# A DFT and two feed-forward layers on one core: six chunks of x have their halves summed by the transfers that load them

## The chip, the core and the metric

The kernel runs on one core of a Trainium2 chip. The metric is the device time of one execution in microseconds (us). The engines go by the names of the profile: PE is TensorE's matmul side and PEld its weight load, DVE is VectorE, ACT ScalarE, POOL GpSimd, SP the SyncE queue from which nearly all transfers are issued. A small q behind a name (SPq, ACTq) is the engine's sequencer, which issues and waits.

## What is computed

x has 2 sequences of 3008 rows of 256 numbers. The output is a real part of a two-dimensional DFT, followed by two feed-forward layers:

```python
X = np.fft.fft(x, axis=1)
X = np.fft.fft(X, axis=2)
x = X.real.reshape(6016, 256)
h = x @ moe_w_in;  x = (h * (1.0 / (1.0 + np.exp(-h)))) @ moe_w_out
h = x @ moe2_w_in; y = (h * np.clip(h + 3.0, 0.0, 6.0) / 6.0) @ moe2_w_out
```

The hidden width of each layer is 2048, and the weights are given in float64.

## The kernel before

**Stages.** The DFT over the 3008 rows is split as 47 x 64. Step 1 (`step1`) does the 47-point part, step 2 the DFT over the 256 columns, step 3 the 64-point part; the result lies in the tile `eo` (even and odd parts). Symmetries are used up ahead of step 1: each row is added to its mirror row, and each half of the columns to the other half and subtracted from it. These adds are called folds here. Then the first layer runs over chunks of 502 tokens (`win1`, `win1_end`, `parts`, `low`), and the second one.

**Chunks of x.** x is loaded in 11 chunks (the table `XCH`, line 60), numbered 0 to 10: 0 to 5 belong to the first sequence, 6 to 10 to the second. Their widths in columns are 1, 2, 4, 4, 4, 2 and 3, 4, 4, 4, 2. A column is 96 rows (48 for each of two halves, spread over partitions) of four parts of 128 numbers, which are the row, its mirror and both with the columns mirrored. `load_x` (line 316) issues one load for chunks 0 and 1 and two for every later one, of 64 and of 32 partitions, all on SP. There are four buffers; chunk i uses buffer i mod 4, and the load of chunk i + 4 is issued behind step 1 of chunk i.

**Folds.** `fold` (line 322) does three operations on VectorE: the first fold adds parts 2 and 3 to parts 0 and 1 (line 325), the second ones make the sum and the difference of parts 0 and 1 (lines 328 and 329). Chunk 2 (`HALF_FOLDED`) has only the first; its second folds are done by TensorE, with two matmuls for each one (lines 349, 350) and a negated table in `t1_sb`. `step1_next` folds chunk i + 1 ahead of the matmuls of chunk i.

**What sets the order.** The order is written out by hand (the schedule is manual): each engine runs its instructions in program order, and semaphores hold it where data are missing. The loop `while i < nx` puts `steps23(g)`, which is step 2 of tile g, step 3 of tile g - 1 and the evacuation of tile g - 2, between the chunks of the second sequence. Then `while g < 14` does the last tiles, and has the first products of the first layer among them. `busy` and the matmuls on `nil` are fillers: they compute nothing that is used.

**Around the change.** The raw float64 weights (`load_raw`, 1 MB each) are issued on SP behind the loads of x. They are decoded on VectorE by `bits_to_float32`, a step at a time, as `advance` gives out time. `split` makes the rounded part `xhi` of a token chunk on ScalarE and puts the rest, `xlo` (line 184, on VectorE), on a list; `do_later` empties it. Before, `do_later` runs in every turn of the last loop right behind `steps23(g)`. In `win1` VectorE makes `z` (`zg`, line 542) of the first product, in `win1_end` it makes `h` (line 553); from g = 8 on it adds to the step 2 tile `o2` (line 387), which step 3 (line 397) reads.

Of the kernel before, what the change touches and what calls it, by code (L numbers as in the profile page):

```python
# [36 lines left out]
F32 = mybir.dt.float32  # L37
# [20 lines left out]
XB = 4  # L58
HALF_FOLDED = 2
XCH = [(0, 0, 1), (0, 1, 2), (0, 3, 4), (0, 7, 4), (0, 11, 4), (0, 15, 2)]  # L60
# [16 lines left out]
def body(tc, xh, x128, t1, t2, t3, w1, w128, w2, out):  # L77
# [227 lines left out]
    w128_raw = fft.tile([P, NF, 2], U32, name="w128_raw")  # L305
    t1_sb = fft.tile([P, 6 * 104], F32, name="t1_sb")
    t2_sb = fft.tile([P, 257], F32, name="t2_sb")
# [5 lines left out]
    xt = {}  # L313
    xbuf = [xp.tile([P, XB, 4 * P], F32, name=f"x{i}", tag=f"x{i}") for i in range(4)]

    def load_x(i):
        n, c, k = XCH[i]
        xt[i] = xbuf[i % len(xbuf)]
        for at in (slice(0, P, 2), slice(1, P, 4)) if i > 1 else (slice(None),):
            nc.sync.dma_start(xt[i][at, :k, :], xh[at, n, c : c + k, :])  # L320

    def fold(i):
        k = XCH[i][2]
        x = xt.pop(i)[:, :k]
        V.tensor_tensor(out=x[:, :, 0:256], in0=x[:, :, 0:256], in1=x[:, :, 256:512], op=ALU.add)
        if i == HALF_FOLDED:
            return x
        V.tensor_tensor(out=x[:, :, 256:384], in0=x[:, :, 0:128], in1=x[:, :, 128:256], op=ALU.add)
        V.tensor_tensor(out=x[:, :, 384:512], in0=x[:, :, 0:128], in1=x[:, :, 128:256], op=ALU.subtract)
        return x  # L330

# [6 lines left out]
    def step1(i, x):  # L338
        n, c, k = XCH[i]
        for h in range(2):  # L340
            ps = psX.tile([P, XB, 96], F32, name="ps1", tag=f"s{h}")
            src = x[:, :, 256 + 128 * h : 384 + 128 * h]
            if SLOTS[c] == 0:
                T.matmul(ps[:, 0, :], src[:, 0], t1_sb[:, 192 + 96 * h : 288 + 96 * h], start=True, stop=False)
                T.matmul(ps[:, 0, 0:48], src[:, 1], t1_sb[:, 384 + 48 * h : 432 + 48 * h], start=False, stop=True)
                k, j = 1, 0
            elif i == HALF_FOLDED:
                for m in range(k):
                    T.matmul(ps[:, m, :], x[:, m, 0:128], t1_sb[:, 96 * h : 96 * h + 96], start=True, stop=False)
                    T.matmul(ps[:, m, :], x[:, m, 128:256], t1_sb[:, 528 * h : 528 * h + 96], start=False, stop=True)  # L350
                j = SLOTS[c]
            else:
                for m in range(k):
                    T.matmul(ps[:, m, :], src[:, m], t1_sb[:, 96 * h : 96 * h + 96], start=True, stop=True)  # L354
                j = SLOTS[c]
            A.activation(
                out1[n][:, h, :, :, j : j + k], ps[:, :k, :].rearrange("p n (s q) -> p q s n", s=2), AF.Copy
            )
# [56 lines left out]
    G.memset(nil, 0.0)  # L415
    G.memset(xbuf[3], 0.0)
    for i in range(2):
        G.memset(xbuf[i][:, XCH[i][2] :], 0.0)
    V.memset(three, 3.0)
# [4 lines left out]
    V.memset(minus, -1.0)  # L424
    V.memset(minus[0:1], 0.0)
    nx = len(XCH)
    for i in range(4):
        load_x(i)
# [8 lines left out]
    def step1_next():  # L437

        nonlocal folded, i
        x = folded  # L440
        if i + 1 < nx:
            folded = fold(i + 1)
        step1(i, x)
        if i + 4 < nx:
            load_x(i + 4)
        if i + 4 == nx - 1:
            load_raw(1, w1, 0)
        i += 1
        if i == 1:
            nc.sync.dma_start(t2_sb, t2)  # L450
            nc.sync.dma_start(t3_sb, t3)
            nc.sync.dma_start(w128_raw, w128)
        if i < HALF_FOLDED + 1:
            busy(3)
        if i == 3:
            V.tensor_tensor(out=xl[:, 0], in0=xl[:, 0], in1=xl[:, 1], op=ALU.add)
        if i == 5:
            step1_last()
        if i == nx - 4:
            load_raw(1, w1, 1)  # L460
            advance(steps, 1)
# [108 lines left out]
    while g < 14:  # L570
        if g < 12:
            steps23(g)
        do_later()
        if g in (7, 10):
# [340 lines left out]
def tables():  # L915
# [6 lines left out]

    t1 = np.zeros((P, 2 * 96 + 2 * 96 + 2 * 48 + 48 + 96))
    r0, r1 = rows()
# [6 lines left out]
    for i in range(2):  # L931
        t1[r0, 480 + 24 * i : 492 + 24 * i] = co[:, i::2]
        t1[r0, 492 + 24 * i : 504 + 24 * i] = si[:, i::2]
        t1[r1, 492 + 24 * i : 504 + 24 * i] = co[:, i::2]
    t1[:, 528:624] = -t1[:, 96:192]
    d, l = np.arange(P), np.arange(P + 1)
# [15 lines left out]
def layout_x(x):  # L952
# [3 lines left out]
    r = rows()  # L956
    xh = np.zeros((P, B, NJ + 1, 4, P), x.dtype)
    xl = np.zeros((P, 2, B, 2, NB // 2), x.dtype)
    for c, j in enumerate(SLOTS):
        for half in range(2 if j < NJ else 1):  # L960
            b = j + NJ * half if j < NJ else NB // 2
            s = (NB * a + NA * b) % S
            for n in range(B):
# [74 lines left out]
```

## Time and profile before

| | us |
|---|---|
| median of 3 runs | 959.12 (959.12 to 960.47) |
| profiled execution | 959.21 |
| its span (first to last instruction) | 957.3 |
| PE busy | 940.8 (98%) |
| DVE busy | 671.4 (70%) |
| ACT busy | 643.6 (67%) |
| POOL busy | 536.7 (56%) |

All times of the trace are counted from the start of the span. A line of the timeline gives the start, the duration (from the first to the last of a group), the engine, the line of the code, the operation, what it writes and reads, and the count. Square brackets tell how long the engine had been idle before it, and what released it. A wait is put down to the release that came last. A float32 matmul appears as two.

### The profile page before, as it was taken

Reading aid. Unit: us, or ns where it says so; the run is one execution under the profiler, and the core shown is the slowest. Engines: PE = TensorE matmul, PEld = TensorE weight load, DVE = VectorE, ACT = ScalarE, POOL = GpSimd, SP = SyncE. Lnnn points to the kernel's source line nnn. Section 1 sums busy time; section 2 is a strip of 40 time slices with the busy share of each in tenths; the row PEclk is TensorE's granted clock in tenths of the full one; section 3 lists DMA queues with packets and bytes.
Section 4 is the critical chain, followed back from the end, with each engine's and each line's share of the span. In section 5 each row is a group of like instructions: output and inputs, shape, how many; then the busy total and the mean of one; then the engine's idle time right before and its main releaser. Section 6 shows DMA issues by size and latency. Waiting matters only on the chain.

```text
span 957.3 us, 12077 instructions
## 1 busy us (share of the span) xinstructions
PE 940.8 (98%) x4292; PEld 778.5 (81%) x4292; DVE 671.4 (70%) x923; ACT 643.6 (67%) x1122; POOL 536.7 (56%) x393
## 2 busy tenths in 40 slices
PE   8999999999999999999999999999999999999998
PEld 8977788888788788888788878888888888888886
DVE  7899999889989897564567675555555555555543
ACT  3777767666656666565677677766776677677665
POOL 1046655646556475465575567754664674576543
PEclk9999999999999999999999999999999999999999
DMA  8433221224252414186400002020020002001001
GB/s 298 170 125 125 92 99 44 99 104 164 83 201 105 158 61 158 64 318 247 150 6 39 1 1 86 1 87 1 1 74 14 1 1 86 1 0 44 1 1 43
DMA packets 20585, 80.23 MB, mean 84 GB/s; under 512 B 2246, under 2 KB 9036, under 8 KB 17900
## 3 DMA queue, kind: packets, MB, share of 16 engines
q1 hardware_dynamic: 20380, 79.14, 22.9%
q8 instruction: 33, 0.54, 0.2%
q10 hardware_dynamic: 144, 0.32, 0.1%
q14 instruction: 28, 0.23, 0.1%
HBM read 50.85 MB, written 28.60 MB: 83 GB/s over the span
## 4 chain that ended last, share of the span: by engine, by line
PE 87%; DVE 8%; issue 3%; ACT 2%; DMA 1%; SPq 0%; DVEq 0%
PE y L295 16%; PE y L297 16%; PE y L296 16%; PE ab L296 4%; PE ab L295 4%; PE ab L297 4%; PE pa L295 3%; PE pa L296 3%; PE pa L297 3%; PE pb L296 2%; PE pb L295 2%; PE pb L297 2%; PE ps L354 1%; PE pc L295 1%; PE pc L296 1%
## 5 line engine op out<-in xcount | busy, mean ns | idle before, releaser
L769 POOL TENSOR_TENSOR glo<-h,ghi 128x502 fp32r<-128x502 f32 (+1 forms) x192 | 250.3, 1315 | 198.7 <-ACT ghi L766 194.9
L604 POOL TENSOR_TENSOR glo<-h,ghi 128x502 fp32r<-128x502 f32 (+1 forms) x144 | 222.7, 1563 | 209.9 <-ACT h L563 180.5
L295 PE MATMUL y<-ghi,whi 128*128 128x502 f32 (+1 forms) x768 | 300.7, 392 | 4.8 <-DVE st L640 2.8
L297 PE MATMUL y<-ghi,wlo 128*128 128x502 f32 (+1 forms) x768 | 300.4, 391 | 0.0
L296 PE MATMUL y<-glo,whi 128*128 128x502 f32 (+1 forms) x768 | 300.4, 391 | 0.0
L295 PEld LDWEIGHTS y<-ghi,whi 128*128 128x128 f32 x768 | 145.3, 189 | 37.5 <-ACT h L563 3.6
L296 PEld LDWEIGHTS y<-glo,whi 128*128 128x128 f32 x768 | 145.4, 189 | 30.7 <-POOL glo L604 0.2
L297 PEld LDWEIGHTS y<-ghi,wlo 128*128 128x128 f32 x768 | 144.9, 189 | 30.2
L766 ACT ACTIVATE ghi<-h 128x502 fp32r<-128x502 f32 (+1 forms) x192 | 118.0, 624 | 49.8 <-DVE h L761 49.8
L562 ACT ACTIVATE ghi<-ab 128x502 fp32r<-128x502 f32 (+1 forms) x96 | 56.6, 590 | 120.9 <-DVE h L553 119.8
L761 DVE SCALAR_TENSOR_TENSOR h<-h,pc 128x502 f32<-128x502 f32 (+1 forms) x96 | 65.1, 678 | 72.2 <-ACT h L758 72.2
L875 DVE TENSOR_TENSOR pc<-u,pb 128x502 f32<-128x502 f32 (+1 forms) x48 | 32.9, 685 | 102.8 <-ACT u L812 102.8
L812 ACT ACTIVATE u<-pa 128x502 f32<-128x502 f32 (+1 forms) x96 | 56.7, 590 | 56.4 <-PE pa L297 55.8
L758 ACT ACTIVATE h<-pc,three 128x502 f32<-128x502 f32 (+1 forms) x96 | 64.6, 673 | 41.7 <-DVE pc L875 37.0
L295 PE MATMUL ab<-xhi,whi 128*128 128x502 f32 (+1 forms) x192 | 75.6, 394 | 1.8 <-DVE zs L542 0.9
L542 DVE SCALAR_TENSOR_TENSOR zs<-eb,w_sb,ab 128x502 f32<-128x502 f32 (+1 forms) x80 | 58.4, 730 | 25.3 <-PE ab L297 25.3
L296 PE MATMUL ab<-xlo,whi 128*128 128x502 f32 (+1 forms) x192 | 75.2, 392 | 0.2 <-DVE xlo L184 0.2
L297 PE MATMUL ab<-xhi,wlo 128*128 128x502 f32 (+1 forms) x192 | 74.9, 390 | 0.0
L758 ACT ACTIVATE h<-pd,three 128x502 f32<-128x502 f32 (+1 forms) x96 | 64.8, 675 | 1.1 <-DVE pd L887 1.1
L761 DVE SCALAR_TENSOR_TENSOR h<-h,pd 128x502 f32<-128x502 f32 (+1 forms) x96 | 64.4, 671 | 0.8 <-ACT h L758 0.8
L563 ACT ACTIVATE h<-h 128x502 f32<-128x502 f32 (+1 forms) x96 | 60.0, 625 | 3.0
L562 ACT ACTIVATE ghi<-h 128x502 fp32r<-128x502 f32 (+1 forms) x96 | 60.2, 627 | 0.0
(173 smaller groups left out, 1586.3 us busy)
## 6 DMA issues: line engine op xcount, KB each, us to landing
raw<-in_w SPq DMA_DIRECT2D x16, 1024.0 KB, 6.5
u<-y_d SPq DMA_DIRECT2D x6, 1004.0 KB, 4.8
part_d<-st SPq DMA_DIRECT2D x5, 1004.0 KB, 4.4
st<-part_d SPq DMA_DIRECT2D x5, 1004.0 KB, 6.4
y_d<-st SPq DMA_DIRECT2D x5, 1004.0 KB, 5.0
out<-st SPq DMA_DIRECT2D x10, 502.0 KB, 3.1
x<-in_xh SPq DMA_DIRECT2D x7, 512.0 KB, 4.6
w2h_d<-h SPq DMA_DIRECT2D x7, 512.0 KB, 2.6
```

The costliest lines, as they stand in the source:

```text
L295: T.matmul(o, wh, xhi, start=first, stop=False, **group)
L296: T.matmul(o, wh, xlo, start=False, stop=False, **group)
L297: T.matmul(o, wl, xhi, start=False, stop=last, **group)
L542: V.scalar_tensor_tensor(out=z[:, :n], in0=eb[:, :n], scalar=w128_sb[:, f : f + 1], in1=ab[:, :n], op0=ALU.mult, op1=ALU.add)
L562: A.activation(ghi[:, s, :n], src, AF.Silu)
L563: A.activation(h[:, s, :n], src, AF.Silu)
L604: eng.tensor_tensor(out=glo[:, s, :n], in0=h[:, s, :n], in1=ghi[:, s, :n], op=ALU.subtract)
L758: A.activation(h[:, i, :n], c[:, :n], AF.Relu, bias=three)
L761: V.scalar_tensor_tensor(out=h[:, i, :n], in0=h[:, i, :n], scalar=6.0, in1=c[:, :n], op0=ALU.min, op1=ALU.mult)
L766: A.activation(g[0][:, i, :n], h[:, i, :n], AF.Copy)
L769: G.tensor_tensor(out=g[1][:, i, :n], in0=h[:, i, :n], in1=g[0][:, i, :n], op=ALU.subtract)
L812: A.activation(t[:, :n], pa[:, :n], AF.Copy)
```

## The change

Chunks 3 to 8 (`SUMMED`) are loaded in two steps. First parts 0 and 1 go into the buffer, then parts 2 and 3 are added to them in SBUF by a transfer with `accum_op=ALU.add`, which GpSimd issues. Such a sum waits until the first half has landed. x is laid out anew in HBM for it, the two halves of a chunk apart. VectorE then does only the second folds of these chunks. They write into the other half of the buffer, so that matmuls read one half and the next load goes into the other. Chunk 2 is folded wholly on VectorE; its doubled matmuls and the negated table go.

Chunks 0 and 1 have small buffers of their own now, and chunks 2 to 10 go around four of full size, so six chunks are under way at the start. The first half of chunk 3 is issued on ScalarE's queue. A third group of filler matmuls stands behind chunk 2. `do_later` runs only at the end of the turns g = 9 and g = 11.

```diff
@@ load_x, fold
-    xbuf = [xp.tile([P, XB, 4 * P], F32, name=f"x{i}", tag=f"x{i}") for i in range(4)]
+    xbuf = [xp.tile([P, 2, k, 2 * P], F32, name=f"x{i}", tag=f"x{i}") for i, k in enumerate((1, 2, *[XB] * 4))]
...
-        xt[i] = xbuf[i % len(xbuf)]
-        for at in (slice(0, P, 2), slice(1, P, 4)) if i > 1 else (slice(None),):
-            nc.sync.dma_start(xt[i][at, :k, :], xh[at, n, c : c + k, :])
+        xt[i] = xbuf[i if i < 2 else 2 + (i - 2) % 4]
+        halves = [slice(0, 1), slice(1, 2)] if i in SUMMED else [slice(0, 2)]
+        for h in halves:
+            for at in (slice(0, P, 2), slice(1, P, 4)) if i > 1 else (slice(None),):
+                dst, src = xt[i][at, slice(0, h.stop - h.start), :k, :], xh[at, n, h, c : c + k, :]
+                if h.start:
+                    G.dma_start(dst, src, accum_op=ALU.add)
+                else:
+                    (A if i == SUMMED[0] else nc.sync).dma_start(dst, src)
...
-        x = xt.pop(i)[:, :k]
-        V.tensor_tensor(out=x[:, :, 0:256], in0=x[:, :, 0:256], in1=x[:, :, 256:512], op=ALU.add)
-        if i == HALF_FOLDED:
-            return x
-        V.tensor_tensor(out=x[:, :, 256:384], in0=x[:, :, 0:128], in1=x[:, :, 128:256], op=ALU.add)
-        V.tensor_tensor(out=x[:, :, 384:512], in0=x[:, :, 0:128], in1=x[:, :, 128:256], op=ALU.subtract)
-        return x
+        x, y = (xt[i][:, h, :k] for h in range(2))
+        if i not in SUMMED:
+            V.tensor_tensor(out=x, in0=x, in1=y, op=ALU.add)
+        V.tensor_tensor(out=y[:, :, 0:128], in0=x[:, :, 0:128], in1=x[:, :, 128:256], op=ALU.add)
+        V.tensor_tensor(out=y[:, :, 128:256], in0=x[:, :, 0:128], in1=x[:, :, 128:256], op=ALU.subtract)
+        return y
@@ step1
-            elif i == HALF_FOLDED:
-                for m in range(k):
-                    T.matmul(ps[:, m, :], x[:, m, 0:128], t1_sb[:, 96 * h : 96 * h + 96], start=True, stop=False)
-                    T.matmul(ps[:, m, :], x[:, m, 128:256], t1_sb[:, 528 * h : 528 * h + 96], start=False, stop=True)
-                j = SLOTS[c]
@@ the start
-    G.memset(xbuf[3], 0.0)
-    for i in range(2):
-        G.memset(xbuf[i][:, XCH[i][2] :], 0.0)
+    G.memset(xbuf[3][:, 0], 0.0)
+    G.memset(xbuf[5], 0.0)
...
+    V.memset(xbuf[4][:, 0], 0.0)
-    for i in range(4):
+    for i in range(6):
         load_x(i)
@@ step1_next
-        if i + 4 < nx:
+        if 2 <= i < nx - 4:
             load_x(i + 4)
...
-        if i < HALF_FOLDED + 1:
+        if i < 4:
             busy(3)
@@ while g < 14
         if g < 12:
             steps23(g)
-        do_later()
...
+        if g in (9, 11):
+            do_later()
         advance(steps, 1700 if g < 8 else 1400)
```

On VectorE, the folds of chunks 2 to 4 before (the tiles x0 to x3 are the four buffers; chunk 4 is in x0):

```order
L325 TENSOR_TENSOR x2_138<-x2_138 128x4x256
L325 TENSOR_TENSOR x3_139<-x3_139 128x4x256
L328 TENSOR_TENSOR x3_139<-x3_139 128x4x128
L329 TENSOR_TENSOR x3_139<-x3_139 128x4x128
L456 TENSOR_TENSOR xl_132<-xl_132 128x128
L325 TENSOR_TENSOR x0_136<-x0_136 128x4x256
L328 TENSOR_TENSOR x0_136<-x0_136 128x4x128
L329 TENSOR_TENSOR x0_136<-x0_136 128x4x128
```

and the same place after it (chunk 4 is in x4):

```order
L332 TENSOR_TENSOR x2_138<-x2_138 128x1024
L333 TENSOR_TENSOR x2_138<-x2_138 128x4x128
L334 TENSOR_TENSOR x2_138<-x2_138 128x4x128
L333 TENSOR_TENSOR x3_139<-x3_139 128x4x128
L334 TENSOR_TENSOR x3_139<-x3_139 128x4x128
L456 TENSOR_TENSOR xl_132<-xl_132 128x128
L333 TENSOR_TENSOR x4_140<-x4_140 128x4x128
L334 TENSOR_TENSOR x4_140<-x4_140 128x4x128
```

Chunk 2 has gained its two second folds, chunks 3 and 4 have lost the first one.

On SP, the loads of chunks 5 to 9 before (buffers x1, x2, x3, x0, x1):

```order
L320 DMA x1_137<-in_xh 64x1024
L320 DMA x1_137<-in_xh 32x1024
L320 DMA x2_138<-in_xh 64x1536
L320 DMA x2_138<-in_xh 32x1536
L320 DMA x3_139<-in_xh 64x2048
L320 DMA x3_139<-in_xh 32x2048
L320 DMA x0_136<-in_xh 64x2048
L320 DMA x0_136<-in_xh 32x2048
L320 DMA x1_137<-in_xh 64x2048
L320 DMA x1_137<-in_xh 32x2048
```

and on GpSimd after it, the sums of chunks 3 to 8 (buffers x3, x4, x5, x2, x3, x4), which stand between its memsets and its first subtractions:

```order
L324 DMA x3_139<-in_xh 64x1024
L324 DMA x3_139<-in_xh 32x1024
L324 DMA x4_140<-in_xh 64x1024
L324 DMA x4_140<-in_xh 32x1024
L324 DMA x5_141<-in_xh 64x512
L324 DMA x5_141<-in_xh 32x512
L324 DMA x2_138<-in_xh 64x768
L324 DMA x2_138<-in_xh 32x768
L324 DMA x3_139<-in_xh 64x1024
L324 DMA x3_139<-in_xh 32x1024
L324 DMA x4_140<-in_xh 64x1024
L324 DMA x4_140<-in_xh 32x1024
```

SP loaded whole chunks, whose rows are twice as long; now it loads the first halves, and GpSimd has twelve transfers that it didn't have.

On VectorE, around the first products of the first layer (42 to 53 us in the trace before), before:

```order
L387 TENSOR_TENSOR o2_526<-ps2_525,xr_133 128x2x129
L184 TENSOR_TENSOR xlo0_517<-eo_75,xhi0_516 128x1004
L126 TENSOR_SCALAR lo1_1_448<-hi1_1_447 128x1024
L128 SCALAR_TENSOR_TENSOR lo1_1_448<-raw_1_1_313,lo1_1_448 128x1024
L387 TENSOR_TENSOR o2_543<-ps2_542,xr_133 128x2x129
...
L387 TENSOR_TENSOR o2_592<-ps2_591,xr_133 128x2x129
L184 TENSOR_TENSOR xlo1_576<-eo_75,xhi1_575 128x1004
L553 SCALAR_TENSOR_TENSOR h_605<-zg0_582,ab_581 128x502
L542 SCALAR_TENSOR_TENSOR zg0_582<-eb0_518,w128_sb_71,ab_611 128x502
```

and after it:

```order
L387 TENSOR_TENSOR o2_532<-ps2_531,xr_133 128x2x129
L126 TENSOR_SCALAR lo1_1_454<-hi1_1_453 128x1024
L128 SCALAR_TENSOR_TENSOR lo1_1_454<-raw_1_1_320,lo1_1_454 128x1024
L387 TENSOR_TENSOR o2_548<-ps2_547,xr_133 128x2x129
L184 TENSOR_TENSOR xlo0_523<-eo_75,xhi0_522 128x1004
...
L387 TENSOR_TENSOR o2_598<-ps2_597,xr_133 128x2x129
L553 SCALAR_TENSOR_TENSOR h_610<-zg0_588,ab_587 128x502
L542 SCALAR_TENSOR_TENSOR zg0_588<-eb0_524,w128_sb_71,ab_616 128x502
L184 TENSOR_TENSOR xlo1_582<-eo_75,xhi1_581 128x1004
```

xlo0 has moved behind the o2 of g = 9, and xlo1 behind the first h and the second zg.

## Rows read from the trace of the kernel before

**Rows 1.** Busy time of each engine over the span, from the page (share, instructions).

```profile
PE 940.8 (98%) x4292; PEld 778.5 (81%) x4292; DVE 671.4 (70%) x923; ACT 643.6 (67%) x1122; POOL 536.7 (56%) x393
```

**Rows 2.** Busy us by stretch: PE, PEld, DVE, ACT, POOL; clock, transfer share, GB/s.

```profile
10.00:14.00 4.00, 3.91 (x36) 3.77 (x34) 2.98 (x5) 0.98 (x2) 0.00 (x0) 1.00 0.90 328
14.00:18.00 4.00, 3.37 (x43) 3.06 (x41) 3.53 (x6) 1.66 (x4) 0.00 (x0) 1.00 0.81 262
18.00:22.00 4.00, 3.91 (x34) 3.67 (x32) 3.84 (x7) 2.29 (x8) 0.00 (x0) 1.00 0.92 307
26.00:30.00 4.00, 4.00 (x39) 4.00 (x38) 3.76 (x7) 2.44 (x8) 0.00 (x0) 1.00 0.99 395
30.00:34.00 4.00, 4.00 (x39) 4.00 (x38) 3.63 (x9) 4.00 (x10) 0.00 (x0) 1.00 0.14 55
38.00:42.00 4.00, 4.00 (x38) 4.00 (x37) 2.96 (x4) 4.00 (x10) 0.00 (x0) 1.00 0.53 200
```

**Rows 3.** Timeline of the start, 1 to 18 us, all engines.

```profile
1.23 1.76 DVE L414 MEMSET x<- 128x2048 f32 x1 [1.23 <-PEq L1026]
...
3.05 0.20 ACT L421 ACTIVATE mask<-three 128x1 f32<-128x1 f32 x1 [0.61 <-DVE three L419]
...
4.74 0.43 DVE L325 TENSOR_TENSOR x<-x 128x256 f32<-128x256 f32 x1 [1.11 <-DMA x<-in_xh]
...
7.95 1.22 DVE L325 TENSOR_TENSOR x<-x 128x1024 f32<-128x1024 f32 x1 [0.45 <-DMA x<-in_xh]
...
8.19 0.86 PE L336 MATMUL psw<-nil 128*128 128x128 f32 x6
...
9.28 0.43 PE L349 MATMUL ps<-t_sb,x 128*128 128x96 f32 x2 [0.23 <-issue]
...
13.15 2.00 PE L354 MATMUL ps<-t_sb,x 128*128 128x96 f32 x16
...
14.98 0.69 DVE L328 TENSOR_TENSOR x<-x 128x512 f32<-128x512 f32 x1
...
15.78 2.00 PE L354 MATMUL ps<-t_sb,x 128*128 128x96 f32 x16 [0.63 <-ACT out L356]
```

**Rows 4.** Loads of x: by size with us to landing; then all 20.

```profile
x<-in_xh SPq DMA_DIRECT2D x1, 192.0 KB, 3.4
x<-in_xh SPq DMA_DIRECT2D x9, 256.0 KB, 4.0
L320 SPq DMA_DIRECT2D x<-in_xh x20: 395/591/1106, 0.7 to 22.2; - x20
DMA to landing us min/median/max: 3.4/4.3/6.1
```

**Rows 5.** Timeline, chunks 6 and 7 and the first weight tile.

```profile
18.19 0.95 DVE L325 TENSOR_TENSOR x<-x 128x768 f32<-128x768 f32 x1
...
23.50 1.92 PE L354 MATMUL ps<-t_sb,x 128*128 128x96 f32 x16
...
29.97 1.14 ACT L110 ACTIVATE lo<-raw 128x1024 f32<-128x1024 f32 x1 [0.44 <-DMA raw<-in_w]
```

**Rows 6.** Timeline of the first products, 42 to 66 us, VectorE and TensorE.

```profile
42.89 1.20 DVE L184 TENSOR_TENSOR xlo<-eo,xhi 128x1004 fp32r<-128x1004 f32 x1
...
46.43 1.13 PE L397 MATMUL ps<-t_sb,o 128*128 128x128 f32 x8 [1.11 <-DVE o L387]
...
47.63 0.39 PE L296 MATMUL ab<-xlo,whi 128*128 128x502 f32 x1
...
48.29 0.74 DVE L542 SCALAR_TENSOR_TENSOR zg<-eb,w_sb,ab 128x502 f32<-128x502 f32 x1 [1.06 <-PE ab L297]
...
51.24 1.06 PE L397 MATMUL ps<-t_sb,o 128*128 128x128 f32 x8
...
53.16 0.49 PE L295 MATMUL ab<-xhi,whi 128*128 128x502 f32 x1 [0.86 <-DVE zg L542]
...
65.48 0.74 DVE L542 SCALAR_TENSOR_TENSOR zs<-eb,w_sb,ab 128x502 f32<-128x502 f32 x1 [1.15 <-PE ab L297]
```

More of the change, by code (lines that the diff above doesn't have):

```diff
@@ L58 @@
 XB = 4
-HALF_FOLDED = 2
+SUMMED = range(3, 9)
 XCH = [(0, 0, 1), (0, 1, 2), (0, 3, 4), (0, 7, 4), (0, 11, 4), (0, 15, 2)]
@@ L305, in body @@
     w128_raw = fft.tile([P, NF, 2], U32, name="w128_raw")
-    t1_sb = fft.tile([P, 6 * 104], F32, name="t1_sb")
+    t1_sb = fft.tile([P, 4 * 96 + 144], F32, name="t1_sb")
     t2_sb = fft.tile([P, 257], F32, name="t2_sb")
@@ L341, in step1 @@
             ps = psX.tile([P, XB, 96], F32, name="ps1", tag=f"s{h}")
-            src = x[:, :, 256 + 128 * h : 384 + 128 * h]
+            src = x[:, :, 128 * h : 128 * h + 128]
             if SLOTS[c] == 0:
@@ L921, in pair @@
         return np.stack([first, second], axis=2).reshape(NA, QA)
-    t1 = np.zeros((P, 2 * 96 + 2 * 96 + 2 * 48 + 48 + 96))
+    t1 = np.zeros((P, 2 * 96 + 2 * 96 + 2 * 48 + 48))
     r0, r1 = rows()
@@ L934, in tables @@
         t1[r1, 492 + 24 * i : 504 + 24 * i] = co[:, i::2]
-    t1[:, 528:624] = -t1[:, 96:192]
     d, l = np.arange(P), np.arange(P + 1)
@@ L956, in layout_x @@
     r = rows()
-    xh = np.zeros((P, B, NJ + 1, 4, P), x.dtype)
+    xh = np.zeros((P, B, 2, NJ + 1, 2, P), x.dtype)
     xl = np.zeros((P, 2, B, 2, NB // 2), x.dtype)
@@ L975, in layout_x @@
                 for part, y, idx in parts:
-                    xh[r[half], n, c, part] = y[:, idx]
+                    xh[r[half], n, part // 2, c, part % 2] = y[:, idx]
                     if idx is minus:
-                        xh[r[half], n, c, part, 0] = 0.0
-    return xh.reshape(P, B, NJ + 1, 4 * P), xl
+                        xh[r[half], n, part // 2, c, part % 2, 0] = 0.0
+    return xh.reshape(P, B, 2, NJ + 1, 2 * P), xl
 def token_columns():
```

## The prediction

> **What bounds the kernel now.** I read the page first: TensorE is busy 98% of the 957.3 us span and VectorE 70% [rows 1]. The change touches only the first 55 us, so the page says little more than this: behind the start the kernel is a TensorE kernel, and whatever TensorE gains or loses in the start should stay to the end. Then the busy time by stretch: in the first four stretches shown, between 10 and 30 us, the transfer engines are busy 81 to 99% of the time and move 262 to 395 GB/s [rows 2]. So the loads of x are themselves near a limit, and a change that gives those engines more to do is not free by default. Third, the start in order of time [rows 3]: chunk 2 lands at 7.95, VectorE folds it once, and TensorE does the second fold by doubled matmuls from 9.28 until chunk 3 follows at 13.15. At 15.78 TensorE has waited 0.63. Chunks 6 to 8 stand in [rows 5]: the matmuls of chunk 7 start at 23.50, without a wait, and the first weight decode waits for its transfer at 29.97. From 18 to 42 us TensorE has next to no idle time, so a chunk that comes late there is a direct loss. Last, the end of the start [rows 6]: TensorE waits 1.11 us at 46.43 for an o2 tile that VectorE makes behind xlo0, and 0.86 at 53.16 for zg, which VectorE makes behind xlo1.
>
> **The change, part by part. Work on VectorE.** The first folds of chunks 3 to 8 go: four of 1.22 (4 columns), one of 0.95 (3 columns), one of 0.69 (2 columns), 6.5 us. Chunk 2 gets two second folds, 0.69 and about the same, 1.4 us [rows 3, 5]. The zeroing of the chunk 4 buffer, half of a 1.76 us memset, or 0.88, falls in the 1.11 us in which VectorE waits for chunk 0, so it is hidden; without that cover it would delay chunk 0 by 0.88 [rows 3]. The relief of 5 us is not on the path: in the start TensorE waits for data and itself.
>
> **TensorE.** Chunk 2 takes 2.00 us (as chunk 3) instead of 13.15 - 9.28 = 3.87. It starts 0.69 later, behind its second fold, and three more filler matmuls follow it, a group of 0.86 (three float32 matmuls are six in the trace). So chunk 3 has its turn at 9.28 + 0.69 + 2.00 + 0.86 = 12.83, 0.3 us earlier than now, and if chunk 4 is there too the 0.63 us wait goes: at most 1.0 us are to be won [rows 3].
>
> **The summing transfers.** No row shows one, nor a transfer issued by GpSimd. The nearest are the plain loads of x: 0.59 us to issue, 3.4 to 6.1 us to landing, median 4.3; the 192 KB pieces 3.4, the 256 KB ones 4.0 [rows 4]. I call the time from issue to landing L. Each chunk of the six now has two of them in a row: first half, landing, GpSimd issues the sum, landing. Chunk 3: the ScalarE queue issues its pieces behind the table load and mask, at 3.3 and 3.9 [rows 3], the sums follow 0.6 apart, so its last sum lands at 3.9 + L + 0.6 + L. Chunk 4 has its first half under way from the beginning as well, and its turn comes 2 us later, so it isn't the tight one. Chunk 7 is: it reuses chunk 3's buffer, so SP holds its load until both second folds (1.37) have read that buffer. Its matmuls can start at 3.9 + 2L + 0.6 + 1.37 + 0.6 + 2L + 0.6 + 0.74 = 7.8 + 4L, the 0.74 being the fold ahead of them. It is wanted at 23.50 [rows 5]. With L = 3.4 it comes 2.1 us early, with 4.3 it is 1.5 late, with 6.1 it is 8.7 late; it is just in time at 3.9. The pieces are now 256 and 128 KB, half of what they were, and a sum has to read what it adds to; I take 3.7 for a plain half and 4.1 for a sum, by the rows of 192 and 256 KB. That gives 23.4: no loss and no gain. Behind SP's wait for chunk 3 stand the loads of chunks 8 to 10 and then the weights, so the same lateness would go on to those. On GpSimd only the first glo stands behind the sums, which needs products of 50 us and later; on ScalarE the evacuation of chunk 0 stands behind its two issues, and chunk 0 isn't folded before 4.74, when these are done [rows 3].
>
> A transfer from GpSimd has its first byte at about 1 us, one from SP or ScalarE at 0.6, says the Trainium skill (DMA: Bandwidth & Descriptors, Latency and other measured facts); no row here shows the former. By it, an estimate, the two sums on chunk 7's path would cost 0.4 us more each and the result would be 0.8 us higher than mine.
>
> **The weights behind them.** The first raw weight tile is issued behind chunk 10, and its user on ScalarE waits 0.44 for it, until 29.97 [rows 5]. ScalarE is busy without a gap from 30 to 34 and from 38 to 42 us, so lateness passes through [rows 2]. The sums add into 21 columns x 96 rows x 1 KB = 2.06 MB. If reading those again costs as much as moving them, that is 5.2 us at the 395 GB/s of 26 to 30 us; what was left unused between 10 and 22 us, (67 + 133 + 88) GB/s x 4 us = 1.15 MB, or 2.9 us, can take some of it [rows 2]. So the bounds are 0 and +2.3 us. I take 0: the loads are issued earlier and fill the gaps that the four buffers left. For the same reason I book no gain of the start: what TensorE wins before 20 us it would wait for at the weights.
>
> **The later xlo.** do_later now runs once after steps23(9) and once behind the products of g = 11. xlo0 goes behind the o2 of g = 9: that o2 is ready 1.11 us earlier (the length of xlo0 on the chain), and TensorE's wait of 1.11 goes. xlo0 itself ends at about 46.25 instead of 44.1, when the first product with xlo0 is due at 46.52 (47.63 - 1.11), so it is hidden; that cover is 0.3 us thick, and what xlo0 is later than that is lost. xlo1 goes behind h and zg. They now start as soon as TensorE has its product, so the 0.86 us wait at 53.16 goes as well. TensorE's last work before it, the step of 51.24, moves by 1.11 and bounds the gain: 1.11 + 0.86 = 1.97, 2.0 us. Does it last? VectorE itself wins only the 1.06 us in which it waited at 48.29. But at 65.48 VectorE waits 1.15 for TensorE, so it is VectorE that has slack there, more than the 0.9 it is behind [rows 6]. I keep 2.0; the bounds are 1.1 (the first wait alone) and 2.2 (with the last of xlo's waits).
>
> **Sum.** The profiled execution took 959.21 us (its span 957.3 and 1.9 around it), the median is 959.12: no difference that matters. 0 for the loads, 0 for the weights, -2.0 for the later xlo: 957.2, and against the median 957.1.
>
> **Rivals.** (a) *Sums as quick as small loads.* With L = 3.4 throughout, all of the 1.0 us of the start stays if the weights also come earlier: 959.1 - 2.0 - 1.0 = 956.1; the smaller pieces and six chunks in flight speak for it, the 90% busy transfer engines against. (b) *The start eats the gain.* L = 4.3 to 4.7, or the full 2.3 us at the weights: +1.5 to +3.1 less 2.0, so 958.6 to 960.2. The median landing speaks for it. (c) *Slower: two landings in series, twice.* The place is chunk 7, behind chunk 3 on one buffer. If plain halves take 4.3 and sums 8.6, chunk 7 is ready at 7.8 + 2 x 4.3 + 2 x 8.6 = 33.6, 10.1 us late, and 959.1 + 10.1 - 2.0 = 967.2. It decides from a mean L of 4.9 (+3.9 less 2.0).  For it: the engines are nearly full as it is. Against it: a landing is mostly time in the queue, and queues get shorter when pieces are halved.
>
> An add in a transfer reads two sources for each write and so runs at half a copy's rate, by the Trainium skill (Collectives: The Full Stack, The bandwidth ceiling: the fold count and why AG ≠ RS ≠ AR). It is the rule that speaks against this change and leads to (c); no row here shows a sum, so nothing yet agrees or disagrees.
>
> **Chances.** Forecast, 956.5 to 957.8: 0.38. (a) 0.24, (b) 0.15, (c) 0.23. A measurement of this kernel can tell about 0.2%, 1.9 us, from no change: the line is at 957.2, in the middle of the forecast. So faster is (a) and half of the forecast, 0.43; within 0.2% the other half and (b), 0.34; slower (c), 0.23. The range runs from 955.0, some way below (a), to 963.0, into the near part of (c); beyond it lie some 0.05 below and 0.12 above.
>
> **What would show it.** In the profile after: o2 and its step3 at about 45.3 without a wait, and no wait for zg at 53 (the 2.0). Chunk 3's matmuls at about 12.8 to 13.2 and chunk 7's at about 23.4, neither behind a wait of VectorE for a sum of more than 0.5 us. L of the sums near 4. ScalarE's wait for the raw tile at 29.97 no longer than 0.44. I am wrong if VectorE waits for sums in chunks 3 to 8 and TensorE idles behind it, or if the gain at 46 and 53 us comes back as new waits for VectorE before 90 us.

## The result and the profile after

The change makes the kernel slower: 965.0 us (964.28 to 965.48) against 959.49 us of the kernel before beside it, a ratio of 1.0055 with an interval of 1.0038 to 1.0073. The forecast was 957.1 with a range up to 963.0, so the time lies outside it, on the side of rival (c). The profiled execution took 964.28 us with a span of 962.5, 5.2 us more than before.

The busy line of the page, against [rows 1]:

```profile
PE 944.5 (98%) x4282; PEld 781.5 (81%) x4282; DVE 667.9 (69%) x920; ACT 643.9 (67%) x1122; POOL 545.1 (57%) x404
```

VectorE has 3.5 us less to do and GpSimd 8.4 us more, as the change says. The next view shows where the time went. It has the stretches of [rows 2] and the same columns (busy us of PE, PEld, DVE, ACT, POOL; granted clock, share of the transfer engines, GB/s):

```profile
10.00:14.00 4.00, 3.27 (x27) 2.91 (x26) 1.61 (x3) 1.00 (x3) 3.51 (x4) 1.00 1.01 210
14.00:18.00 4.00, 2.53 (x18) 2.56 (x18) 2.79 (x5) 0.51 (x2) 0.00 (x0) 0.85 0.97 221
18.00:22.00 4.00, 4.00 (x40) 3.88 (x39) 0.94 (x3) 1.71 (x4) 3.51 (x4) 0.72 0.84 214
22.00:26.00 4.00, 2.88 (x22) 2.46 (x22) 1.03 (x2) 1.71 (x6) 1.71 (x2) 1.00 0.98 207
```

The transfer engines are as busy as before or busier (1.01 and 0.97 against 0.90 and 0.81), yet they move 210 and 221 GB/s where it was 328 and 262. TensorE is idle for 1.5 us of the second stretch and 1.1 us of the fourth, and between 14 and 22 us its granted clock is below 1.00 on average. The same in order of time, against [rows 3] and [rows 5] (start, duration, engine, line, operation; in brackets the idle time ahead of it and its releaser):

```profile
9.09 1.23 DVE L332 TENSOR_TENSOR x<-x 128x1024 f32<-128x1024 f32 x1 [1.56 <-DMA x<-in_xh]
...
11.14 2.00 PE L354 MATMUL ps<-t_sb,x 128*128 128x96 f32 x16 [0.57 <-issue]
...
14.63 0.69 DVE L333 TENSOR_TENSOR x<-x 128x512 f32<-128x512 f32 x1 [2.99 <-DMA x<-in_xh]
...
15.47 5.41 PE L354 MATMUL ps<-t_sb,x 128*128 128x96 f32 x32 [1.63 <-DVE x L333]
...
23.93 0.56 DVE L333 TENSOR_TENSOR x<-x 128x384 f32<-128x384 f32 x1 [2.55 <-DMA x<-in_xh]
...
24.63 1.55 PE L354 MATMUL ps<-t_sb,x 128*128 128x96 f32 x12 [1.12 <-DVE x L333]
...
26.81 0.69 DVE L333 TENSOR_TENSOR x<-x 128x512 f32<-128x512 f32 x1 [1.85 <-DMA x<-in_xh]
...
27.83 1.92 PE L354 MATMUL ps<-t_sb,x 128*128 128x96 f32 x16
...
34.26 1.19 ACT L110 ACTIVATE lo<-raw 128x1024 f32<-128x1024 f32 x1
```

The trace before has for the matmuls of chunks 6 and 8:

```profile
20.37 1.48 PE L354 MATMUL ps<-t_sb,x 128*128 128x96 f32 x12
...
27.07 1.92 PE L354 MATMUL ps<-t_sb,x 128*128 128x96 f32 x16
```

Read the lines after the change from the top: chunk 2's first fold (7.95 before), its matmuls (9.28), chunk 3's fold and its matmuls with those of chunk 4 (13.15), chunk 6's fold and matmuls (20.37), chunk 7's (23.50), and the first weight decode (29.97). Every fold of a summed chunk waits for its transfer. The lateness is 1.9 us at chunk 2, 2.3 at chunk 3, and 4.3 at chunks 6 and 7. From there it is handed on: the product `y` that begins 240 us into the trace before comes about 5 us later, and the last one of the kernel 4.9 us later.

The transfers themselves, against [rows 4]: issue times in ns (shortest, median, longest), first and last start, and the time from issue to landing. L324 are the sums, L326 the plain loads:

```profile
L324 POOL DMA_DIRECT2D x<-in_xh x12: 842/1090/1842, 7.3 to 23.8; - x12
...
  DVE x L333: 11.3, 6
...
DMA to landing us min/median/max: 5.0/5.9/7.4
...
L326 SPq DMA_DIRECT2D x<-in_xh x18: 455/571/742, 0.7 to 26.7; - x18
...
DMA to landing us min/median/max: 2.7/4.7/6.0
```

The second line says who waited for the sums: VectorE's second folds, six times, 11.3 us in all. Last, what each queue's packets cost in the first 45 us (packets, MB, share of 16 engines' time; q0 is GpSimd's queue, q1 that of SP; ScalarE's is a third one, with 0.66 MB):

```profile
q1 hardware_dynamic: 2800, 7.52, 46.7%
q0 software_dynamic: 768, 2.07, 26.5%
```

A plain MB takes 6.2% of the engines' time in this stretch, a summed one 12.8%, 2.06 times as much. The Trainium skill (Collectives: The Full Stack, The bandwidth ceiling: the fold count and why AG ≠ RS ≠ AR) says of the add in a collective that it needs two source reads and runs at about half a copy's rate, and the trace agrees for this add. The new layout of x costs no engine time by itself: before, SP's queue took 66.8% for 10.63 MB, 6.3% for one.

### The profile page after: what moved, and what is told of

The parts are those of the page before. It is cut to its first block, busy times and chain, and to the rows that moved or that the text cites. A ratio compares the mean times of both kernels' runs of the same rounds, so it can differ in the third digit from the quotient of the medians.

```text
span 962.5 us, 12083 instructions
## 1 busy us (share of the span) xinstructions
PE 944.5 (98%) x4282; PEld 781.5 (81%) x4282; DVE 667.9 (69%) x920; ACT 643.9 (67%) x1122; POOL 545.1 (57%) x404
## 3 DMA queue, kind: packets, MB, share of 16 engines
q0 software_dynamic: 768, 2.07, 1.2%
## 4 chain that ended last, share of the span: by engine, by line
PE 86%; DVE 8%; issue 2%; DMA 2%; ACT 1%; POOL 0%; DVEq 0%; POOLq 0%
PE y L295 16%; PE y L296 16%; PE y L297 16%; PE ab L295 4%; PE ab L296 4%; PE ab L297 4%; PE pa L295 3%; PE pa L296 3%; PE pa L297 3%; PE pb L296 2%; DMA x<-in_xh 2%; PE pb L295 2%; PE pb L297 2%; PE pc L295 1%; PE pc L296 1%
```

## The experiments

The theory after this profile: the sums take longer to land and take the engines twice as long, and chunks 6 and 7, which need two such round trips in a row, come 4.3 us late. The rivals: GpSimd's queue is slow whatever it carries; the reuse of four buffers is the trouble; six chunks under way at once delay the one that is needed first; TensorE's lower clock adds to it; and the order of `xlo` costs something on its own.

### The sums apart from their add

```diff
-                    G.dma_start(dst, src, accum_op=ALU.add)
+                    G.dma_start(dst, src)
```

> The changed kernel with the twelve GpSimd transfers as plain copies: they overwrite the first half, so the first fold of chunks 3 to 8 is left out; issue, waits and sizes stay. Theory A (a summed byte costs the transfer engines twice a plain one, and they are full): the GpSimd queue takes per MB about what SP's takes (6.2% of the first 45 us instead of 12.8%), landings fall from 5.9 to about 4.3, chunk 7's matmuls start near 25 instead of 27.83, total about 960. Theory B (the delay is that of two landings in series and of GpSimd's slow issue, whatever the transfer does): landings stay above 5 us, chunk 7 stays near 27.5, total 964 to 965.

Measured: 960.85 us (959.6 to 963.55), a ratio of 1.0028 [1.0019, 1.0037]. Its queue in the first 45 us, the issues with their landing, and the matmuls of chunk 6:

```profile
q0 software_dynamic: 672, 2.07, 14.3%
...
L324 POOL DMA_DIRECT2D x<-in_xh x12: 537/549/702, 7.2 to 22.3; - x12
...
DMA to landing us min/median/max: 3.5/4.2/5.3
...
22.77 1.55 PE L354 MATMUL ps<-t_sb,x 128*128 128x96 f32 x12 [1.09 <-DVE x L333]
```

The same 2.07 MB on the same queue cost 14.3% of the engines without the add and 26.5% with it, a factor of 1.85; they land after 4.2 us instead of 5.9 and are issued in 0.55 us instead of 1.09. So the engine time is that of the add, not of GpSimd's queue. But chunk 6 is still 2.4 us late (22.77 against 20.37), and chunk 7, at 25.97, comes between the two forecasts of 25 and 27.5: some half of the loss is there without any add. The two landings in series and the six chunks under way are left in this kernel.

### The whole change without the new order of xlo

```diff
         if g < 12:
             steps23(g)
+        do_later()
...
-        if g in (9, 11):
-            do_later()
```

> The changed kernel with do_later in its old place. If the move is worth 2.0 us in the changed kernel: 967. If it is given back there: 965 to 965.5, with the waits for o2 (1.1) and zg (0.9) back at about 50 and 57 us and the wait of 1.39 at 61.76 gone.

Measured: 964.93 us, a ratio of 1.0072 [1.006, 1.0085]; the interval overlaps that of the whole change. TensorE's line for chunk 6, and a stretch behind it:

```profile
24.60 2.26 PE L354 MATMUL ps<-t_sb,x 128*128 128x96 f32 x12 [2.08 <-DVE x L333]
...
26.00:28.00 2.00, 2.00 (x12) 2.00 (x11) 1.15 (x2) 0.54 (x3) 0.00 (x0) 0.50 1.04 307
```

Chunk 6's matmuls start as in the changed kernel, and the products are 5.9 us late from the first one on. So the start alone makes the loss. This profile shows one thing more. The folds of chunk 7 begin when they did (26.85 against 26.81), but its matmuls start at 29.43, 1.6 us later than in the changed kernel: TensorE had done chunks 3 and 4 at full clock, waited 2.08 us for chunk 6 instead of 1.12, and behind this wait its clock fell to 0.50.

### The new order of xlo alone

```diff
         if g < 12:
             steps23(g)
-        do_later()
...
+        if g in (9, 11):
+            do_later()
         advance(steps, 1700 if g < 8 else 1400)
```

> The kernel before with do_later moved as in the change, and nothing else. If the move is worth the 2.0 us that were forecast: 957.5, with no wait of TensorE at 46.4 and 53.2. If VectorE's lateness takes it back a step further on (TensorE waits for the z of the third product, which before the change was ready only 0.3 us ahead of its use at 57.02): 958.5 to 959.5, with a new wait of 0.5 to 1.5 us at about 57.

Measured: 959.05 us against 958.66, a ratio of 1.0001 [0.9993, 1.001]. The lines of VectorE and TensorE that answer to [rows 6]:

```profile
45.29 1.13 PE L397 MATMUL ps<-t_sb,o 128*128 128x128 f32 x8
...
52.06 1.75 DVE L116 TENSOR_SCALAR lo<-lo 128x1024 f32<-128x1024 f32 x1
...
56.00 0.72 DVE L542 SCALAR_TENSOR_TENSOR zg<-eb,w_sb,ab 128x502 f32<-128x502 f32 x1
...
56.78 0.50 PE L295 MATMUL ab<-xhi,whi 128*128 128x502 f32 x1 [1.39 <-DVE zg L542]
```

Step 3 starts at 45.29 without a wait, as forecast, and the wait for `zg` at 53 us is gone; the products that began at 53.16 begin at 51.09, 2.07 us earlier. Then the gain is given back at once: TensorE waits 1.39 us for the `zg` of the third tile, which begins at 56.00 as it did before (55.98). VectorE does the same row of work up to there, and its L116 takes 1.75 us where it took 0.69, since GpSimd's first `glo` now begins at 51.64, ahead of it, and not at 53.64.

### The weight decode behind it moved one turn later

```diff
-        advance(steps, 1700 if g < 8 else 1400)
+        advance(steps, 1700 if g < 8 else {11: 0, 12: 2800}.get(g, 1400))
```

> The kernel before with the later do_later, and the decoding steps of turn g = 11 (lines 116 and 118, 1.75 and 1.64 us beside GpSimd's subtraction) moved into turn g = 12, behind the z of the third product. If it was these steps ahead of z that gave the 2.0 us back: no wait of TensorE at about 57, and 957 to 958. If VectorE's work as a whole bounds the stretch up to 85 us: the wait comes back as longer waits for zs at about 70 to 76 us, and 958.5 to 959.5.

This edit goes on top of the one above. Measured: 958.59 us against 958.3, 1.0002 [0.9993, 1.0011]. In TensorE's timeline the wait has moved once more:

```profile
55.12 0.47 PE L295 MATMUL ab<-xhi,whi 128*128 128x502 f32 x1
...
61.59 0.50 PE L296 MATMUL y<-glo,whi 128*128 128x502 f32 x1 [1.20 <-DVE glo L605]
```

The third tile's product comes without a wait and 1.9 us earlier than before (55.12 against 57.02), but 6 us later TensorE waits 1.20 us for a `glo` that VectorE makes. I had expected it at 70 to 76 us. That VectorE's whole work bounds this stretch, and not the place of one tile in its row, fits this, but one place tried doesn't show it.

### Buffers of their own for chunks 6 to 8

```diff
-    xbuf = [xp.tile([P, 2, k, 2 * P], F32, name=f"x{i}", tag=f"x{i}") for i, k in enumerate((1, 2, *[XB] * 4))]
+    xbuf = [xp.tile([P, 2, k, 2 * P], F32, name=f"x{i}", tag=f"x{i}") for i, k in enumerate((1, 2, *[XB] * 7))]
...
-        xt[i] = xbuf[i if i < 2 else 2 + (i - 2) % 4]
+        xt[i] = xbuf[i if i < 2 else 2 + (i - 2) % 7]
...
+    for b in xbuf[6:]:
+        G.memset(b[:, 0], 0.0)
```

> The changed kernel with seven full buffers instead of four, so the loads of chunks 6 to 8 wait for no fold. Theory A (engine time): the same bytes go through the same full engines; chunk 8's matmuls still start 3 us or more later than before the change, total 964 to 965. Theory B (series of landings through the reused buffer): chunks 6 to 8 are there in time behind chunk 5, only the 3.0 us at the first step 2 stay, total 962 to 963.

Measured: 964.59 us, 1.0068 [1.0054, 1.0082]. The landing of its sums, and the matmuls of chunk 6:

```profile
DMA to landing us min/median/max: 6.0/7.3/9.6
...
24.14 1.55 PE L354 MATMUL ps<-t_sb,x 128*128 128x96 f32 x12 [0.83 <-DVE x L333]
```

Chunk 6 no longer waits for a buffer, but the sums take 7.3 us instead of 5.9, and it comes only 0.5 us earlier. That was the reading on which my formula for chunk 7 rested (two round trips through one buffer), and taking it away helps by no more than this: what is issued earlier takes longer to land.

### Six chunks under way without a sum

```diff
-SUMMED = range(3, 9)
+SUMMED = range(0)
...
-                    (A if i == SUMMED[0] else nc.sync).dma_start(dst, src)
+                    (A if i == 3 else nc.sync).dma_start(dst, src)
...
```

The buffers of chunks 3 to 5 are zeroed whole on GpSimd for it.

> The changed kernel without sums: all chunks are loaded whole from SP (chunk 3 from ScalarE's queue) and folded twice on VectorE; six chunks under way, chunk 2 wholly on VectorE and the later do_later stay. If all of the loss comes with the sums (their engine time and their place behind a first landing): 958 to 959.5, the first step 2 at 18.5 to 19.2, chunk 7 at 23 to 23.5. If six chunks in flight or chunk 2 on VectorE do harm of their own: 960 to 962, with the first step 2 after 20.

Measured: 961.88 us (960.9 to 964.21), 1.0045 [1.0029, 1.006]. Its timeline for chunks 2 and 6, and one stretch:

```profile
9.95 1.22 DVE L332 TENSOR_TENSOR x<-x 128x1024 f32<-128x1024 f32 x1 [2.42 <-DMA x<-in_xh]
...
12.00 2.00 PE L354 MATMUL ps<-t_sb,x 128*128 128x96 f32 x16 [1.39 <-issue]
...
21.70 1.48 PE L354 MATMUL ps<-t_sb,x 128*128 128x96 f32 x12
...
14.00:18.00 4.00, 3.33 (x29) 3.16 (x29) 3.97 (x7) 1.47 (x3) 0.00 (x0) 1.00 0.50 151
```

Chunk 2 lands 2.0 us later than before (9.95 against 7.95) and its matmuls begin 2.7 us later, although nothing is summed; 0.69 of this is the second fold that VectorE now does for it. The transfers that are early leave the engines half idle from 14 to 18 us, so nothing is won by it. By chunk 6 1.3 us of the lateness are left. Six chunks under way, started like this with chunk 3 on a second queue, are a loss of their own here.

### Chunk 3 behind chunk 2 on SP's queue

```diff
-                    (A if i == SUMMED[0] else nc.sync).dma_start(dst, src)
+                    nc.sync.dma_start(dst, src)
```

> The changed kernel, but the first half of chunk 3 is issued by SP behind chunk 2 and no longer by ScalarE's queue beside it. Theory A (chunk 3's early transfer shares the engines with chunk 2, which lands about 1.1 us later for it): chunk 2's first fold starts near 8.0 again (9.09 in the changed kernel, 7.95 before) and its matmuls near 10.0, but chunk 3's sums are then issued later, so chunk 3's matmuls stay between 15.0 and 16.5 and chunk 7's between 27.5 and 28.5; the time stays at 964 to 966. Rival (the queue of ScalarE is not the cause, the other transfers in flight are): chunk 2's fold stays above 8.8. Rival (the lateness of chunk 2 is what the whole loss starts from): chunk 3's matmuls come at about 14.4 and the time falls to about 963.5.

Measured: 966.9 us (966.06 to 970.18), 1.0098 [1.0077, 1.0118], slower than the change itself and than the 964 to 966 that I had. VectorE's and TensorE's lines for chunks 2 and 3:

```profile
7.98 1.23 DVE L332 TENSOR_TENSOR x<-x 128x1024 f32<-128x1024 f32 x1 [0.50 <-DMA x<-in_xh]
...
16.67 0.69 DVE L333 TENSOR_TENSOR x<-x 128x512 f32<-128x512 f32 x1 [6.13 <-DMA x<-in_xh]
...
17.51 6.37 PE L354 MATMUL ps<-t_sb,x 128*128 128x96 f32 x32 [4.78 <-DVE x L333]
```

Chunk 2 is back at 7.98, so it was chunk 3's load on the second queue that took its share. But then chunk 3 lands for VectorE at 16.67, 2.0 us later than in the change, and TensorE waits 4.78. I had chunk 3's matmuls at 16.5 at the latest and chunk 7's at 28.5; they start at 17.51 and 30.10. The two round trips of a summed chunk leave no place for it: started early it harms chunk 2, started late it harms itself.

### Half of the sums

The list of summed chunks is cut to chunks 3 to 5 in the one kernel and to 6 to 8 in the other:

```diff
-SUMMED = range(3, 9)
+SUMMED = range(3, 6)
```

> The changed kernel with sums for chunks 3 to 5 alone; 6 to 8 are loaded whole. The first step 2 stays near 22.1, 3.0 us late, since chunk 3 has its two landings as in the change. If lateness in the start is kept and not made up: 961.5 to 963. If chunks 6 to 8 come late too because the transfer engines are behind: 963 to 965.

```diff
-SUMMED = range(3, 9)
+SUMMED = range(6, 9)
...
```

In the second one chunk 3, now whole, stays on ScalarE's queue, and the buffers are zeroed as in the kernel without a sum.

> The changed kernel with sums for chunks 6 to 8 alone; 3 to 5 are loaded whole. 11 of 21 summed columns stay. If the added engine time decides (about 3 us of it stays, in a stretch that had 2.9 us unused): 959 to 961, chunk 6 within 1 us of its old start. If it is the two landings in series behind a reused buffer: chunks 6 and 7 come 2 us late or more, 961 to 962.5.

Measured: 961.63 us, 1.0034 [1.0021, 1.0048], for chunks 3 to 5, and 964.05 us, 1.0057 [1.0043, 1.007], for chunks 6 to 8. The matmuls of chunk 6 in the first and in the second, and those of chunk 8 in the second:

```profile
22.48 1.48 PE L354 MATMUL ps<-t_sb,x 128*128 128x96 f32 x12
...
23.31 1.55 PE L354 MATMUL ps<-t_sb,x 128*128 128x96 f32 x12 [0.59 <-DVE x L333]
...
31.36 2.00 PE L354 MATMUL ps<-t_sb,x 128*128 128x96 f32 x16 [1.11 <-DVE x L333]
```

Chunk 6 is 2.1 and 2.9 us late, 4.3 with all six sums and 1.3 with none. At chunk 8 the two differ more: 2.1 us late in the first kernel (29.19) and 4.3 in the second, where TensorE waits a second time; 4.6 with all six sums (31.70) and 1.3 with none (28.40). So the sums of chunks 6 to 8 make nearly the whole lateness by themselves, and their time lies above both ranges that I had for it, 959 to 962.5. The sums of chunks 3 to 5 add 0.8 us at either chunk, but no time that can be told from that of the kernel without a sum (961.63 against 961.88).

### More fillers ahead of the gaps

```diff
-            busy(3)
+            busy({2: 5, 3: 8}.get(i, 3))
```

> The changed kernel with five more filler matmuls behind chunk 2 and two more behind chunk 1, so that TensorE doesn't idle 1.63 us at 15.47, behind which its granted clock was 0.50 from 18 to 20 us and the 32 matmuls of chunks 3 and 4 took 5.41 us instead of 4.0. Theory A (what is late at chunk 6 is its data, the clock costs only what would be waited out there): the granted clock stays at 1.00 between 16 and 20 us, chunks 3 and 4 take 4.0, chunk 5 and step 2 come about 1.4 us earlier, but chunk 6's matmuls stay at 24.3 to 24.9 behind a longer wait for VectorE's fold, and the time stays at 964 to 966. Rival (the lower clock is part of the loss): chunk 6's and 7's matmuls come 1.0 to 1.4 us earlier and the time is about 963.6.

Measured: 966.41 us, 1.0084 [1.0067, 1.0101]. The matmuls of chunk 6, and two stretches:

```profile
25.38 2.50 PE L354 MATMUL ps<-t_sb,x 128*128 128x96 f32 x12 [2.77 <-DVE x L333]
...
18.00:22.00 4.00, 4.00 (x45) 3.63 (x46) 1.37 (x4) 1.74 (x5) 3.30 (x4) 1.00 0.86 204
...
26.00:30.00 4.00, 4.00 (x24) 4.00 (x24) 1.29 (x2) 1.41 (x5) 0.13 (x1) 0.60 0.96 248
```

The granted clock stays at 1.00 between 14 and 22 us, and the first step 2 begins at 21.22 instead of 22.12. TensorE then waits 2.77 us for chunk 6 instead of 1.12, and behind that wait its clock falls to 0.60. So what is done faster ahead of chunk 6 is waited out at chunk 6; the lower clock ahead of it isn't the cause. Chunk 6 itself comes 0.75 us later than in the change, and later than the 24.9 that I had at most; why its sum landed later isn't known. That the kernel is slower still, where I had 964 to 966, agrees with a clock that now falls where no wait follows: chunk 6's twelve matmuls take 2.50 instead of 1.55, and chunk 7's start at 30.21, 2.4 us later than in the change, though its fold begins as early (26.89).

### Chunk 2 folded on VectorE, nothing else

```diff
-        if i == HALF_FOLDED:
-            return x
...
-            elif i == HALF_FOLDED:
+            elif i < 0:
```

> The kernel before with one part of the change: chunk 2 has its second folds on VectorE and not by doubled matmuls on TensorE; loads, buffers and the order of xlo are those of before. My prediction's step (at most 1.0 us are to be won at the start) says: chunk 3's matmuls near 12.8 and chunk 4's up to 1.0 us earlier than 15.78, time 958.1 to 958.6. Rival (chunk 3 and 4 wait for their folds on VectorE, which chunk 2's two second folds of 0.69 stand ahead of): chunk 3's matmuls between 12.9 and 13.2 and chunk 4's at 15.7 to 15.8, and the time is that of before within 0.1%.

This one is made from the kernel before. Measured: 958.05 us against 958.45, 1.0 [0.999, 1.0009]. VectorE's first fold of chunk 3, and its matmuls:

```profile
11.20 1.23 DVE L325 TENSOR_TENSOR x<-x 128x1024 f32<-128x1024 f32 x1 [0.49 <-DMA x<-in_xh]
...
13.36 2.00 PE L352 MATMUL ps<-t_sb,x 128*128 128x96 f32 x16 [1.15 <-ACT out L354]
```

Chunk 3's matmuls start at 13.36 and chunk 4's at 15.99, 0.2 us later than before, though TensorE has 1.9 us less to do. The wait of 1.15 is put down to ScalarE's evacuation, but the fold of chunk 3 that the matmuls read ends at 13.15, just ahead of them, 0.2 us later than before. Ahead of its first fold VectorE still waits 0.49 for the transfer. Before it waited 1.81 there:

```profile
10.99 1.23 DVE L325 TENSOR_TENSOR x<-x 128x1024 f32<-128x1024 f32 x1 [1.81 <-DMA x<-in_xh]
```

So chunk 3 is bound by its landing and its folds, and not by what TensorE or VectorE does for chunk 2. The doubled matmuls of the kernel before were free.

## Why the prediction was wrong

**What bounds the start: right in kind.** "The loads of x are themselves near a limit" was the second thing that I read, and it is what decides. I didn't carry it into the sum, though: there the transfers had a latency each and no share of a common limit. Both signs of being wrong that I had named came: TensorE idles behind VectorE's waits for sums, and the gain at 46 and 53 us comes back as a new wait before 90.

**The landing of a sum: the failed term.** The forecast was that chunk 7's matmuls can start at 7.8 + 4L, with 3.7 for a plain half and 4.1 for a sum. On its path the trace after has: chunk 3's second piece issued at 3.64 (I had 3.9), its sum issued at 8.76 and landed at 14.51, which is 5.75 us; chunk 7's second piece issued at 16.52 and landed at 19.22, 2.7 us; its sum issued at 20.03 and landed at 26.68, 6.65 us. The sums took 5.75 + 6.65 = 12.4 instead of 8.2, 4.2 us more. The plain halves and their issues were 0.8 us longer the first time and 0.8 shorter the second, so they even out. Chunk 7's lateness is 4.3. On this path the form of the calculation held and one number in it was wrong: I priced the add by the smaller piece of a plain load, when a row of plain loads can't bound what an add does. The break-even that rival (c) named, a mean L of 4.9, was met: (4.5 + 5.75 + 2.7 + 6.65) / 4 = 4.9, the 4.5 being taken from the issue of the sum behind it.

**The place: not chunk 7 alone.** I worked out chunk 7 and passed over chunk 6, which stands behind chunk 2's buffer. With my own values it has 7.95 + 1.22 + 1.37 + 0.6 + 3.7 + 0.6 + 4.1 + 0.6 = 20.1 against 20.37, as little slack as chunk 7. It is the one that TensorE waits for (1.12 at 24.63); chunk 7 then follows it in TensorE's order. And the run with seven buffers shows that the buffer alone isn't what holds either of them. On chunk 6's path the sum was not the largest error. Chunk 2's fold came 1.1 us late, the sum took 5.0 instead of 4.1 (18.78 to 23.80), and the second piece of the plain half, issued at 12.20, took 6.0 instead of 3.7:

```profile
L326 SPq DMA_DIRECT2D x<-in_xh x1: 602/602/602, 12.2 to 12.2; - x1
...
DMA to landing us min/median/max: 6.0/6.0/6.0
```

In the run without the add the same piece is issued at 12.23 and lands after 3.7 us, and the transfer that stands for its sum takes 5.1. So here the add acts through the plain load, which is under way together with the sums of chunks 4 and 5. What failed is thus the step that gave each transfer a landing time of its own: a sum also lengthens what shares the engines with it.

**Chunk 2 as a fixed point: wrong.** The step "it starts 0.69 later" took chunk 2's landing at 7.95 for granted. With chunk 3 on a second queue it lands at 9.09. I had written of ScalarE's queue only what stands behind it there, not that its transfer shares the engines with the one that is needed first. Chunk 3's turn came at 15.47 and not at 12.83: 2.2 us of this are its own two landings, the last at 14.51 instead of 12.3.

**A gain of at most 1.0 in the start: nothing.** It counted TensorE's own work; the run with only that part shows that chunk 3's landing and folds bound its place already, so nothing was to be won there.

**The weights at 0: right, but not for its reason.** ScalarE's first decode has no wait at all at 34.26, against 0.44 before. I had the loads issued earlier; the first weight load is issued at 27.34 instead of 22.81, 4.5 us later. It costs nothing because all that stands ahead of the decode is 4.3 us late as well, so the zero is luck.

**The later xlo at -2.0: right for 5 us, then nothing.** Both waits went: the products came 1.14 us earlier and then 2.07 with the new order alone, against 1.11 and 1.97 in the forecast. The step that failed is "does it last?". I looked for slack at 65.48, but the `zg` of the third tile is needed at 57.02 and ended at 56.70 before, a slack of 0.3 us. VectorE's row up to it holds the same work in both orders, so it couldn't come earlier. In the changed kernel the same row of lines reads:

```profile
50.27 1.13 PE L397 MATMUL ps<-t_sb,o 128*128 128x128 f32 x8
...
60.98 0.72 DVE L542 SCALAR_TENSOR_TENSOR zg<-eb,w_sb,ab 128x502 f32<-128x502 f32 x1
...
61.76 0.49 PE L295 MATMUL ab<-xhi,whi 128*128 128x502 f32 x1 [1.39 <-DVE zg L542]
```

The lateness of the products is 3.8 us before 52 us, 2.9 at 56 us and 4.7 at 61.76.

**Rival (c): right mechanism, at half its price.** It had 8.6 us for a sum and a loss of 10.1; the sums took 5.9 in the median and the loss at chunk 7 is 4.3. The add doubles the engine time, but not the landing: 5.9 us against 4.2 for the plain copy of the same pieces is 1.4 times. Its chance of 0.23 was too low: the argument against it, "queues get shorter when pieces are halved", left out that the bytes weren't halved, and that the summed half of them costs double.

**What stays open.** The runs split the loss at chunk 6 into some 1.3 us for six chunks under way, some 1.1 for the second landing in series (the kernel without the add has 2.4) and some 1.9 for the add, each taken as a difference of single profiles, in which chunk starts of like kernels differ by some tenths. How much of the 1.3 is chunk 3's place on the second queue isn't told apart. The spans of single profiles differ by more, and not because of the start. In every profile TensorE waits some 1.9 us for `st`, which VectorE makes, between the layers, at about 263 us of the trace before. Behind this wait the granted clock falls to 0.50 for some 3 us in eight of the thirteen profiles and stays at 1.00 in the other five. One stretch of the kernel before and of the one with chunk 2 folded alone:

```profile
264.00:266.00 2.00, 2.00 (x6) 1.61 (x5) 2.00 (x4) 0.18 (x1) 1.58 (x2) 0.50 0.16 68
...
264.00:266.00 2.00, 2.00 (x10) 1.64 (x10) 2.00 (x4) 0.24 (x1) 1.65 (x2) 1.00 0.15 64
```

The second kernel's products come 0.2 us later than before ahead of this wait and 1.5 us earlier behind it. So the lateness is better read ahead of it: at 254 us it is 5.0 us in the changed kernel, 4.8 with the sums of chunks 6 to 8, 2.6 without the add, 2.3 with the sums of chunks 3 to 5 and 1.6 without sums. Why the kernel without sums then has a median 3.6 us longer than before isn't settled: two of its four executions agree with its profile (960.9), the other two took 962.84 and 964.21 and have none.

## What to carry to other kernels

Where transfers already fill their engines, an add in a transfer isn't a free add: it saves VectorE a microsecond that nobody waited for and costs engine time that the other loads wait for too. Before work is moved to a resource, read that resource's share in the stretch in question, and price the moved work by the engine time of its bytes, and what that adds to the loads beside it, not by the latency of a like instruction. And when a wait is removed by a new order on one engine, go through that engine's next results one by one up to the first that is used without slack; the gain lasts only until there.

## What the runs showed of the hardware

- A byte that is summed into SBUF costs the transfer engines about twice a plain one: 26.5% against 14.3% of their time for the same 2.07 MB on the same queue. It lands later too (5.9 against 4.2 us), and GpSimd takes 0.84 to 1.84 us to issue it, against 0.54 to 0.70.
- In the run without the add, pieces of 256 and 128 KB from GpSimd land after 4.2 and 4.1 us in the median, and pieces of these sizes from SP after 3.3 and 3.1. Only one and three of SP's landings are in the trace, and they were issued at other moments, so that GpSimd's land later isn't shown. The Trainium skill (DMA: Bandwidth & Descriptors, Latency and other measured facts) has the first byte of a transfer from GpSimd at about 1 us and of one from SP at about 0.6; these landings neither confirm nor exclude it.
- Near the start of the kernel, a transfer on a second queue takes its share from one that was issued earlier: chunk 2's fold starts at 7.98 when chunk 3 stands behind it, at 8.75 to 9.13 beside half of chunk 3, and at 9.95 and 10.17 beside the whole of it.
- An idle TensorE can pay twice. Behind waits of 1.63 and 4.78 us the granted clock stood at 0.50 (1.2 GHz of 2.4) for stretches of 2 and 4 us, and 32 matmuls took 5.41 and 6.37 us instead of 4.0; with fillers in the first gap it stayed at 1.00 there. Behind 2.08 us of waiting at chunk 6 it cost the next chunk 1.6 us. The same wait doesn't always do it: behind the 1.9 us between the layers the clock fell in eight profiles of thirteen, which is worth some 1.6 us of the whole time.
- VectorE's L116 takes 0.69 us alone and 1.75 beside GpSimd's subtraction. The Trainium skill (SBUF — State Buffer, SBUF: two separate sides) tells of a port pair that the two engines lock against each other for a whole instruction, and the trace agrees: the 1.06 us more are about what was left of the first of GpSimd's two subtractions (3.30 us for both, from 51.64) when L116 began at 52.06.
